# Attention in 64-row and 64x64 TensorE tiles, with compact states, slot-major tokens and a new instruction planner

## The chip, the cores and the metric

The kernel runs on one core of one Trainium2 chip. The metric is the device time of one execution in microseconds (us). The kernel before takes 210.27 us, the median of three runs (209.99 to 210.47).

Five engines work side by side, each through its own instructions in a fixed order: TensorE (PE; its weight loads are listed apart as PEld), VectorE (DVE), ScalarE (ACT), GpSimd (POOL) and SyncE (SP). In this kernel SP issues the loads of the inputs and the stores of the output, and POOL's queue issues the loads of the weights. Within one engine the instructions run in the order in which the program lists them, so an instruction whose input is late holds back every instruction behind it, whatever those need. (In the trace of before, shown below, a product that was ready at 36.99 us ran at 47.10 us for that reason.)

## The reference, cut to what matters

```python
# q, k, v, alpha: (B=4, H=8, S=768, D=48) fp32; alpha between 0.8 and 1.0
for t in range(S):
    state = alpha[:, :, t, :, None] * state + k_t (outer) v_t
    y[:, :, t] = q_t @ state
x = y as (B, 768 tokens, 384 columns)
h = relu(x.T @ w_tok1) @ w_tok2            # 768 -> 256 -> 768, along the tokens
u = x + h.T
out = u + relu(u @ w_ch1) @ w_ch2          # 384 -> 1536 -> 384, along the columns
```

## The kernel before: the parts that matter

The recurrence is computed in 12 chunks of 256 tokens, three to each of the four batches. A chunk is held as 128 pairs of tokens (64 pairs in each half), so that "slot 0" and "slot 1" are the even and the odd token of each pair. For each chunk the kernel forms running products of alpha (a cumulative sum of logarithms on TensorE, then exponentials on ACT, giving `E` and `IE`), scales q and k by them (`pkq`, `pkk`), transposes both, forms masked scores (`gtm`) and multiplies them by v ("y"). "K" is the product of k and v that updates the state, and "inter" adds to y what the state of earlier tokens gives. After three chunks the mixer of that batch can run: t1, t2, u, transposes of u, then 72 TensorE products c1, 72 products c2, the output tiles `o` and their stores.

The order is not written by hand. A planner on the host, a list scheduler, keeps a clock for each engine. It repeatedly takes the instruction that could start first, with a priority that decides between those that could start at about the same time. It knows the data's landing only through a model:

```python
    def run(self):                                     # class Plan
        ...
            if o.dma is not None:
                kind, dur, lead, tail = o.dma
                if kind == "w":                        # a weight transfer
                    s = max(st + lead, dma_w)
                    dma_w = s + dur
                    if dma_free > s:
                        dma_free += dur
                    else:
                        dma_free = max(dma_free, s) + 0.9 * dur
                else:                                  # a load of q, k, v or alpha
                    s = max(st + lead, dma_free)
                    dma_free = s + dur
                o.end = (dma_w if kind == "w" else dma_free) + tail
        ...
IN_NS, OUT_NS = 1450.0, 560.0
CLASSES = {... "vt": 5, "acqm": 2, "tmp": 2, "ss": 4, "rt": 24, "o": 4,
           "one": 4, "pair": 2}                        # PSUM: 4 single banks, 2 pairs
```

The operations that the change touches:

```python
    def tr(self, bank, cls, v):                        # q or k of one chunk: 8 transposes of 128x128
        for sl in range(2):
            for j in range(4):
                c = (sl * 4 + j) * 128
                self.pe.transpose(o[:, c : c + 128], s[:, sl, 2 * j : 2 * j + 2, :], self.idn)

    def evq(self, e, tpq, bq):                         # brings the two slots back into token order
        self.copy(e, self.t(tpq).rearrange("p j (t s) -> p s j t", s=2), ...)

    def kmm(self, kp, pkk, vb, nst):                   # two heads at a time: half of each result is unused
        ... self.bank(kp, hf)[:, 96 * j : 96 * j + 96], lhsT=kk[ph, sl, 2 * j : 2 * j + 2, :], ...

    def sadd(self, t, kp, s0, hf):                     # states are 384 columns wide
        self.nc.vector.tensor_tensor(self.t(t), self.bank(kp, hf)[:, 0:HD], self.t(s0), ALU.add)

    def inter(self, yp, tpq, s, hf):                   # acqm has zeroed the unused half
        for j in range(4):
            self.pe.matmul(self.bank(yp, hf)[:, 96 * j : 96 * j + 96],
                           lhsT=self.t(tpq)[:, j, hf * 128 : hf * 128 + 128],
                           rhs=self.t(s)[:, 96 * j : 96 * j + 96], ...)

    def store(self, o, b, i):
        self.nc.sync.dma_start(self.out[b, i * 128 : (i + 1) * 128, :], self.t(o))
```

## Time and profile before

| where in the trace of before | us |
|---|---|
| span of the profiled execution | 209.3 |
| start of the first channel product c1 (L702) | 58.7 |
| from there to the first t1 of batch 1 ("first mixer") | 27.4 |
| to the first t1 of batch 2 ("second mixer") | 48.2 |
| to the first t1 of batch 3 ("third mixer") | 39.5 |
| from there to the end of the span | 35.5 |

I read these five stages off the timeline of TensorE. The last four each hold one mixer's channel products (in before, 12 of the first mixer's 144 fall into the stage after it).

These lines are from the page of before. The first gives busy time and instructions. The others cut the span into 40 slices of 5.2 us; a digit is the busy share of a slice in tenths, PEclk is the clock granted to TensorE in tenths, and the last line is what the DMA engines moved.

```profile
PE 171.1 (82%) x2004; PEld 108.9 (52%) x2004; DVE 128.3 (61%) x200; ACT 98.0 (47%) x184; POOL 62.1 (30%) x66
PE   0367466119999999976888998999999999999993
PEclk9999976755999999999699999999999999999999
DMA  6999999999999997223001000211000112200042
GB/s 175 325 325 315 203 208 203 205 272 301 262 320 269 288 261 226 75 76 79 0 3 53 25 37 28 90 38 41 3 0 3 39 39 77 75 3 0 0 150 75
```

TensorE is nearly full from slice 10 on. Before that it is not, and two slices (37 to 47 us) have it at a tenth. The rate of the DMA engines falls from 325 to about 205 GB/s in slices 5 to 8, just when the weights move. Split by queue (the DMA view of the trace from 20.9 to 41.9 us), these slices hold so many packets, MB, and so much of the engines' time:

```profile
q0 software_dynamic: 3659, 3.05, 89.9%
q1 hardware_dynamic: 3225, 1.22, 33.1%
```

q0 carries the weights and q1 the loads. Both moved nearly the same number of packets, but a packet of weights is larger (about 830 against 380 bytes), so over these 21 us the loads are left with 58 GB/s of their 325. The 205 GB/s do not mean that the engines read less. The weights are counted by the bf16 bytes that are written (3.15 MB in all), while they are read as fp32: of the 25.17 MB that the page says were read from HBM, the 48 loads of 384 KB are 18.87, which leaves 6.29 MB for the weights. An estimate from these figures is 2 x 145 + 58, about 350 GB/s read. What fell is the share of the loads.

The granted clock is 5 to 7 tenths in slices 6 to 10, in and around the hole: the eight transposes at 46.13 us below take 1.04 us, those of a later, busy stage (113.57 us) 0.62 us.

Next, the chain of waits of before, followed back from the last instruction (start, length, what):

```profile
19.88 7.01 SPq L493
26.93 18.11 DMA qt<-in_q_dram
...
182.28 11.87 PE ps L702 x72
194.16 11.71 PE ps L707 x72
```

The chain waits for one q tile until 45.04 us. In its last part it is nothing but TensorE at 162 to 165 ns a product (11.71 us and 11.87 us over 72). No new order can shorten that part.

The timeline of before shows why so little happened from 37 to 47 us. Columns are start, length, engine and line, what was done, how many, and in brackets how long the engine had been idle and what ended that.

```profile
34.63 2.36 DVE L614 TENSOR_TENSOR gtm<-ps,mk 128x1024 bf16<-128x1024 f32 x2 [3.61 <-PE ps L606]
...
37.54 0.99 POOL L519 TENSOR_TENSOR at<-at 128x384 f32<-128x384 f32 x1 [11.08 <-DMA at<-in_alpha_dram]
...
43.32 0.99 POOL L545 TENSOR_TENSOR kt<-kt,at 128x384 f32<-128x384 f32 x1 [4.79 <-DMA kt<-in_k_dram]
...
44.27 1.80 POOL L553 TENSOR_TENSOR pkq<-qt,E 128x768 bf16<-128x768 f32 x1
...
46.03 2.13 POOL L553 TENSOR_TENSOR pkk<-kt,IE 128x768 bf16<-128x768 f32 x1
...
46.13 1.04 PE L586 MATMUL ps<-idn,pkq 128*128 128x128 bf16 x8 [6.33 <-POOL pkq L553]
...
46.41 2.57 DVE L553 TENSOR_TENSOR pkk<-kt,IE 128x768 bf16<-128x768 f32 x1
...
47.10 0.82 PE L650 MATMUL ps<-vb,gtm 64*128 64x48 bf16 x32
```

The masks of the third chunk are ready at 36.99 us (34.63 + 2.36), and its y (L650) needs nothing more that is late. It runs at 47.10. In TensorE's order it stands behind the q transposes of the fourth chunk. Those wait for POOL's `pkq`, and POOL stood for 11.08 and then 4.79 us on loads of the *fifth* chunk. The fifth chunk's alpha and k were put in front of the fourth chunk's work in POOL's order, because the planner believed that they would land earlier than they did.

The two `pkk` products at 46.03 and 46.41 show a second effect. VectorE's takes 2.57 us here; the shortest of its kind in this trace takes 0.94 us. It ends 0.82 us after POOL's. The Trainium skill, "SBUF — State Buffer", section "Who interferes with whom", says that a VectorE instruction with two inputs in SBUF contends with a GpSimd instruction that reads SBUF, and calls the port pair that they share an exclusive lock. These two lines agree with it for VectorE: its product ends about its own 0.94 us after POOL's, as if it had waited for POOL to finish. POOL's, at 2.13 us, is longer than the 1.80 us of its `pkq` too, but spans on POOL are rough.

### The profile page before, as it was taken

How to read it: one execution, taken by the hardware profiler on the slowest of the kernel's cores; microseconds unless marked ns; L12 is line 12 of the kernel's file. 1: busy time of each engine (PE TensorE's matmuls, PEld its weight loads, DVE VectorE, ACT ScalarE, POOL GpSimd, SP SyncE). 2: the span in 40 equal slices, each digit the busy share in tenths (PEclk: the TensorE clock that was granted, in tenths of full speed). 3: DMA queues.
4: the chain of work that ended last, by engine and by line, in shares of the span. 5: the costliest groups of instructions: out<-in, count | busy, mean ns of one | idle time of the engine just before them, and what ended most of it. 6: DMA issues, size and time to landing. Idle time of an engine off the chain costs nothing.

```text
span 209.3 us, 4761 instructions
## 1 busy us (share of the span) xinstructions
PE 171.1 (82%) x2004; PEld 108.9 (52%) x2004; DVE 128.3 (61%) x200; ACT 98.0 (47%) x184; POOL 62.1 (30%) x66
## 2 busy tenths in 40 slices
PE   0367466119999999976888998999999999999993
PEld 0246253016665666643545555656666666666551
DVE  2899973038999639289648968569645372800211
ACT  4474313516472750281577732146987301199200
POOL 4469700179372060075306031053800000000000
PEclk9999976755999999999699999999999999999999
DMA  6999999999999997223001000211000112200042
GB/s 175 325 325 315 203 208 203 205 272 301 262 320 269 288 261 226 75 76 79 0 3 53 25 37 28 90 38 41 3 0 3 39 39 77 75 3 0 0 150 75
DMA packets 57221, 27.04 MB, mean 129 GB/s; under 512 B 50416, under 2 KB 57200, under 8 KB 57200
## 3 DMA queue, kind: packets, MB, share of 16 engines
q1 hardware_dynamic: 53376, 23.60, 40.7%
q0 software_dynamic: 3824, 3.15, 9.3%
q8 instruction: 15, 0.25, 0.5%
q14 instruction: 6, 0.05, 0.1%
HBM read 25.17 MB, written 4.72 MB: 143 GB/s over the span
## 4 chain that ended last, share of the span: by engine, by line
PE 58%; DVE 15%; SPq 12%; DMA 9%; issue 3%; ACT 2%; DVEq 0%; ACTq 0%
PE ps L707 21%; PE ps L702 20%; SPq L493 12%; DMA qt<-in_q_dram 9%; PE ps L678 3%; PE ps L586 3%; DVE pkk L553 3%; DVE u L687 3%; DVE gtm L614 3%; PE ps L650 2%; PE ps L606 2%; PE ps L683 1%; PE ps L624 1%; PE ps L656 1%; DVE o L711 1%
## 5 line engine op out<-in xcount | busy, mean ns | idle before, releaser
L702 PE MATMUL ps<-ut,wc 128*128 128x384 bf16 x288 | 52.2, 331 | 1.1 <-ACT ut L590 0.3
L707 PE MATMUL ps<-wc,rt 128*128 128x384 bf16 x288 | 52.8, 326 | 0.0
L673 ACT ACTIVATE rt<-ps 128x384 bf16<-128x384 f32 x79 | 38.5, 494 | 13.9 <-PE ps L702 13.8
L702 PEld LDWEIGHTS <-wc 128*128 128x128 bf16 x288 | 27.2, 99 | 20.4 <-issue 3.9
L707 PEld LDWEIGHTS <-rt 128*128 128x128 bf16 x288 | 26.8, 98 | 16.8
L711 DVE TENSOR_TENSOR o<-ps,u 128x384 f32<-128x384 f32 x24 | 13.2, 555 | 32.6 <-PE ps L707 29.2
L614 DVE TENSOR_TENSOR gtm<-ps,mk 128x1024 bf16<-128x1024 f32 x24 | 28.7, 1217 | 3.7 <-PE ps L606 3.6
L590 ACT COPY tpq<-ps 128x1024 bf16<-128x1024 bf16 x11 | 14.4, 1309 | 13.7 <-PE ps L586 13.7
L574 POOL TENSOR_TENSOR acqm<-E,bm 128x16 f32<-128x16 f32 x12 | 9.0, 751 | 35.8 <-PE ps L683 12.0
L553 POOL TENSOR_TENSOR pkq<-qt,E 128x768 bf16<-128x768 f32 x6 | 10.8, 1806 | 20.8 <-ACT E L538 20.8
L590 ACT CAST x<-ps 128x384 bf16<-128x384 f32 x13 | 6.1, 485 | 22.9 <-PE ps L656 18.3
L586 PE MATMUL ps<-idn,pkq 128*128 128x128 bf16 x96 | 9.0, 249 | 8.1 <-POOL pkq L553 6.3
L687 DVE TENSOR_TENSOR u<-ps,x 128x384 bf16<-128x384 f32 x24 | 12.5, 551 | 4.5 <-PE ps L683 4.5
L678 PE MATMUL ps<-x,wt 128*128 128x384 bf16 x48 | 11.4, 373 | 4.4 <-ACT x L590 2.4
L532 PE MATMUL ps<-la,u 128*128 128x384 bf16 x12 | 4.8, 399 | 10.0 <-DVE u L473 6.0
L553 POOL TENSOR_TENSOR pkk<-kt,IE 128x768 bf16<-128x768 f32 x6 | 12.4, 2068 | 0.2 <-ACT IE L541 0.2
L606 PE MATMUL ps<-tpq,tpk 48*64 48x128 bf16 x384 | 10.9, 240 | 1.8 <-DVE tmp L638 1.0
L586 PEld LDWEIGHTS <-pkq 128*128 128x128 bf16 x96 | 7.2, 112 | 9.3 <-POOL pkq L553 6.4
L675 DVE TENSOR_SCALAR rt<-ps 128x384 bf16<-128x384 f32 x17 | 8.6, 556 | 5.4 <-PE ps L702 5.4
L592 DVE COPY tpk<-ps 128x1024 bf16<-128x1024 bf16 x11 | 7.6, 690 | 7.0 <-PE ps L586 7.0
L650 PE MATMUL ps<-vb,gtm 64*128 64x48 bf16 x384 | 8.0, 188 | 4.5 <-DVE gtm L614 4.4
L586 PE MATMUL ps<-idn,pkk 128*128 128x128 bf16 x96 | 9.0, 251 | 3.3 <-DVE pkk L553 2.0
(68 smaller groups left out, 225.8 us busy)
## 6 DMA issues: line engine op xcount, KB each, us to landing
at<-in_alpha_dram SPq DMA_DIRECT2D x12, 384.0 KB, 5.0
kt<-in_k_dram SPq DMA_DIRECT2D x12, 384.0 KB, 5.1
qt<-in_q_dram SPq DMA_DIRECT2D x12, 384.0 KB, 4.8
vt<-in_v_dram SPq DMA_DIRECT2D x12, 384.0 KB, 5.7
out_dram<-o SPq DMA_DIRECT2D x24, 192.0 KB, 1.9
wc<-in_moe_w_ch_dram POOLq DMA_DIRECT2D x3, 384.0 KB, 13.7
wc<-in_moe_w_ch_dram POOLq DMA_DIRECT2D x2, 576.0 KB, 17.9
wt<-in_moe_w_tok_dram POOLq DMA_DIRECT2D x2, 384.0 KB, 9.2
```

The costliest lines, as they stand in the source:

```text
L493: self.ins[id(v)] = self.nc.sync.dma_start(self.t(v), src)
L553: self.eng[e].tensor_tensor(dst[:, :, :, 0:D], src.rearrange("p h s d -> p s h d"), bass.AP(tensor=f.tensor, offset=f.offset, ap=[list(f.a ...
L586: self.pe.transpose(o[:, c : c + 128], s[:, sl, 2 * j : 2 * j + 2, :], self.idn)
L590: self.act.copy(d, s)
L606: self.pe.matmul(self.bank(gp, r)[hf * 64 : hf * 64 + 64, j * 128 : j * 128 + 128], lhsT=tk[r * 64 : r * 64 + D, sl * 4 + j, hf * 64 : hf ...
L614: self.nc.vector.tensor_tensor(self.t(gtm)[:, sl, :, :], pr, bass.AP(tensor=m.tensor, offset=m.offset, ap=[list(m.ap[0]), [0, 8], [1, 128] ...
L673: self.act.activation(d, s, AF.Relu)
L678: self.pe.matmul(self.bank(bank)[:, 0:HD], lhsT=self.wt1[:, kc, m * 128 : m * 128 + 128], rhs=self.t(x), start=(kc == 0), stop=(kc == NS - 1))
L687: self.nc.vector.tensor_tensor(self.t(u), self.bank(bank)[:, 0:HD], self.t(x), ALU.add)
L702: self.pe.matmul(self.bank(bank)[:, 0:HD], lhsT=self.wc1[:, kc, mc * 128 : mc * 128 + 128], rhs=self.t(ut)[:, kc, half * 384 : half * 384 ...
L707: self.pe.matmul(self.bank(bank)[:, 0:HD], lhsT=self.t(rts[mc][0])[:, i * 128 : i * 128 + 128], rhs=self.wc2[:, mc, :], start=(mc == 0), s ...
L711: self.nc.vector.tensor_tensor(self.t(o), self.bank(bank)[:, 0:HD], self.t(u), ALU.add)
```

## The change: its intent, and the diff

The stated intent is to do the attention products and transposes of the token pairs as 64-row or 64x64 TensorE tiles. A 64x64 tile of TensorE can compute one head alone, so that K no longer computes the unused cross terms of two heads. The states then need 192 columns instead of 384, and `acqm` (which zeroed the cross terms) goes. q stays in slot-major order, so its eviction from PSUM becomes contiguous. In return the tokens of x, and so of the output tiles, come in slot-major order: the rows of `wt1` and the columns of `wt2` are permuted, and each output tile is stored in two half-height transfers.

The diff holds more than that. It also replaces the planner. Cut to its core:

```diff
+    def landed(self, s, need):                 # a load advances at W_SHARE of its rate
+        ...                                    # while weights move
+            room = (b - t) * W_SHARE
     def run(self):
+        for _ in range(3):                     # plan, note when weights move, plan again
+            self.once()
...
-            if kind == "w": ...                # the model shown above
+            if kind == "w":
+                s = max(st + lead, dma_w); dma_w = s + dur
+                self.wnew.append((s, dma_w)); o.end = dma_w + tail
+            else:
+                dma_free = self.landed(max(st + lead, dma_free), dur)
+                o.end = dma_free + tail
+                    elif o.port and port_by != e and port > st and (e == "DVE" or e == "POOL"):
+                        st = port              # "port": products of VectorE and POOL exclude each other
...                                            # a model of TensorE's cold and warm clock; other slack
+W_SHARE = 0.19
-IN_NS, OUT_NS = 1450.0, 560.0
+IN_NS, OUT_NS = 1215.0, 560.0
-    "vt": 5, "acqm": 2, "tmp": 2, "ss": 4, "o": 4, "one": 4, "pair": 2,
+    "vt": 4,            "tmp": 3, "ss": 5, "o": 3,     # singles and pairs share the 8 PSUM banks
+WIDE = (0, 1, 2)        # batch 0: one 768-wide cumulative sum; no products P, k0a, q0r
...
     def tr(self, bp, v):
+        for c in range(8):
+            for hf in range(2):                # 16 transposes of 64x64
+                self.pe.transpose(o[:, c * 64 : c * 64 + 64], s[ph, c % 2, c - c % 2 : c - c % 2 + 2, :],
+                                  self.idn[ph, ph])
-    def inter(self, yp, tpq, s, hf): ...
+    def inter(self, yp, tpq, states, flip):    # one head per product, 64-row tiles
+                hf = r ^ flip                  # flip 0 and flip 1: each row tile changes the PSUM bank
+    def fence(self, e, yp):                    # a tiny read of PSUM between flip 0 and flip 1
+        self.copy(e, self.junk[e], self.pair(yp)[:, :, 7 * D - 1 : 7 * D + 1])
...
     def store(self, o, b, i):
+        dst = self.out[b, i * 128 : (i + 1) * 128, :].rearrange("(t s) d -> s t d", s=2)
+        for h in range(2):
+            self.nc.sync.dma_start(dst[h], self.t(o)[64 * h : 64 * h + 64, :])
```

The fence is there because of what the Trainium skill, "TensorEngine Tiling (Array Packing)", section "Restrictions and Gotchas", Gotcha 1, states: different row tiles cannot access the same PSUM bank at the same time. Leaving it out would be a race.

## The prediction

> **What bounds the kernel now.** In the chain of waits, the first 58.7 us hold almost no TensorE link: load issues by the sync queue to 26.9 us, then one DMA wait (a q tile) to 45.1 us. From 58.7 us on the chain is TensorE nearly without a break (L702 and L707, 41% of the span), with one bad stretch, 89 to 118 us, full of VectorE links.
>
> The prologue is a head-of-line loss more than a bandwidth limit. In the timeline the third chunk's masks end at 37.0 us, but its y product (L650) runs at 47.1: in TensorE's order it stands behind the fourth chunk's q transposes, whose input POOL made only at 44.27, after sitting (L519 at 37.5, L545 at 43.3) on loads of the *fifth* chunk. Those are late because the weights move too: the 40-slice row gives 325 GB/s before and about 205 from 21 to 42 us. The Trainium skill, "DMA: Bandwidth & Descriptors", on arbitration, says each engine round-robins between queues; the trace agrees.
>
> **What the change does.** The built order shows that the planner has changed, not only the tiles. Before the first channel product TensorE now needs only chunks 0 to 3; before, chunk 3 had landed by about 30 us. ACT's second ut eviction stands behind one load of chunk 4 (37.5 us before). Batch 0 loses nine products (P, k0a, q0r; 0.55 to 1.1 us each). After chunk 3 come transposes, t1, ht, t2 on a cold clock, then about 7 us of VectorE (six u at 0.55, q0r, qq, a tpq). I expect the first channel product (L702 before) at about 43 us instead of 58.7: minus 15 us, nearly all critical.
>
> TensorE per chunk, warm: transposes 2 x 0.45 us become 2 x 0.32 (20 ns for 64 columns, interpolated between y, 16 ns at 48, and K, 28 ns at 96); K 0.44 to 0.5; inter 0.34 to 0.26; one more change of tiling. "TensorEngine Tiling (Array Packing)", Key Properties, says a mode change drains; here three products cost 0.59 instead of 0.49 us after attention: 0.1 us each. Net about 0.2 us x 8 chunks: minus 1.5 us.
>
> VectorE: state adds 0.55 to 0.33, multiplies 0.64 to 0.38, tpq eviction 1.30 (strided) to 0.69, on ACT 1.31 to 1.02; acqm (9 us of POOL) goes; fences come (0.1 us each, plus waiting). Some 8 us less, of which perhaps 4 count, in the second mixer: from its t1 to the next batch's t1 before spent 48 us, against 39.5 for the following one. Eight shared PSUM banks help there too.
>
> Costs: permuting wt2 (two ACT copies, hidden), split stores (tail 0.4 us longer), TensorE stalls at the fence (0 to 0.5 us a chunk).
>
> Sum: 210.3 - 15 - 1.5 - 4 = 189.8; I say **189 us**, range **181 to 198**. Chances: faster 0.97, same 0.02, slower 0.01.
>
> **What would show it.** Right: first channel product at 40 to 47 us; y of the third chunk before 36; second mixer 40 to 45 us; transposes about 20 ns apart, under 0.35 us a group; POOL busy under 45 us; final channel stretch as before. Wrong: TensorE waiting on chunk 4's loads before the first channel product; transposes no faster; TensorE gaps before inter's second half.
>
> **What would make it wrong.** If weights (wt1 in two half-height transfers) or chunk 3's loads land later, the prologue gain shrinks to 8 us. If denser VectorE work or the fences stall TensorE, 5 us return. If the second mixer runs as the third, 183 us.

## The result, and the profile after

The median is 191.77 us (190.72 to 191.84, four runs) against 210.16 us for before (four runs by then). The ratio is 0.911, with a 95% interval of 0.908 to 0.915. Ratios in this document compare the runs of one kernel with the runs of the other in the same rounds, so they are not quite the ratio of the medians that I quote. Executions over 1.5% slower than the fastest of the same kernel are left out of the means.

The same five stages in both traces:

| | before | after | difference |
|---|---|---|---|
| first c1 starts at | 58.7 | 40.9 | -17.8 |
| first mixer | 27.4 | 32.5 | +5.1 |
| second mixer | 48.2 | 40.6 | -7.6 |
| third mixer | 39.5 | 39.0 | -0.5 |
| last stage | 35.5 | 37.1 | +1.6 |
| span | 209.3 | 190.1 | -19.2 |

From the page of after:

```profile
PE 164.0 (86%) x2489; PEld 101.7 (53%) x2489; DVE 112.8 (59%) x197; ACT 101.2 (53%) x200; POOL 35.9 (19%) x43
PE   0578578769999988977999999989999999999990
PEclk9999999978999999999999999999999999999997
DMA  5999999999999998999100123110001132000243
GB/s 156 322 320 270 240 209 207 205 203 270 283 295 247 288 299 229 298 264 269 47 3 3 41 54 75 41 47 5 3 0 40 46 86 71 12 3 0 65 100 83
```

The hole at 37 to 47 us is gone. Slices are 4.75 us here, so TensorE is nearly full from 43 us on, and the granted clock dips in two slices only, besides the last. The rate of about 205 GB/s while the weights move has stayed. The loads did not become faster; the order stopped depending on the late ones.

From the timeline of after, the lines that answer to those of before:

```profile
30.53 0.57 PE L617 MATMUL ps<-vb,gtm 64*128 64x48 bf16 x32
...
39.65 0.52 ACT L605 ACTIVATE lf<-at 128x384 f32<-128x384 f32 x1 [2.11 <-DMA at<-in_alpha_dram]
...
40.08 0.78 ACT L683 COPY ut<-ps 128x768 bf16<-128x768 bf16 x1
...
40.91 4.11 PE L794 MATMUL ps<-ut,wc 128*128 128x384 bf16 x15 [1.24 <-ACT ut L683]
```

The third chunk's y runs at 30.53 instead of 47.10 us. The first channel product still waits a little for a load: ACT's `ut` copy stands behind its own first step on the next batch's alpha.

The chain of waits of after:

```profile
20.53 19.10 DMA at<-in_alpha_dram
40.91 4.11 PE ps L794 x15
...
64.83 6.69 DMA at<-in_alpha_dram
...
161.54 11.87 PE ps L794 x72
173.41 11.71 PE ps L799 x72
```

The last two lines are the same as before to the digit. The wait at 64.83 is new. It lies in the first mixer, the stage that became 5.1 us longer. But only a third of these 5.1 us is waiting. These two lines give the first mixer in before and in after, from the view of busy time by stretch: its bounds, its length, the busy time of PE, PEld, DVE, ACT and POOL with the count of instructions, the granted clock, and the DMA engines' share and GB/s:

```profile
58.68:86.12 27.44, 27.40 (x322) 17.06 (x317) 21.05 (x36) 11.59 (x22) 8.22 (x8) 1.00 0.93 255
40.91:73.42 32.51, 30.83 (x468) 18.24 (x468) 22.88 (x39) 23.09 (x49) 7.43 (x9) 0.95 1.05 270
```

TensorE was busy for 27.40 of 27.44 us and is now busy for 30.83 of 32.51, so 1.7 us are waiting and 3.4 us are longer work. Both stages hold 132 channel products. The first 15 of them in after, at a lower granted clock, took 4.11 us (274 ns each, where the last 72 took 165): that is about 1.7 us. The other 1.7 us or so are attention products that stood before the first c1 and now stand behind it; y of the fourth chunk, for one, runs at 44.96. (The two halves of the 3.4 us are estimates from these figures.) At the first t1 of batch 1 the gain is thus 12.7 us (86.12 less 73.42), not 17.8. The timeline of after shows the waiting, and one wait of the second mixer:

```profile
71.61 0.52 ACT L605 ACTIVATE lf<-at 128x384 f32<-128x384 f32 x1 [3.55 <-DMA at<-in_alpha_dram]
72.04 0.14 ACT L683 COPY junkACT<-ps 128x4 f32<-128x4 f32 x1
...
72.23 0.28 PE L617 MATMUL ps<-ss,tpq 48*128 48x48 bf16 x8 [1.68 <-ACT junkACT L683]
...
85.70 0.56 DVE L803 TENSOR_TENSOR o<-ps,u 128x384 f32<-128x384 f32 x1 [1.79 <-DMA out_dram<-o]
...
86.32 0.66 PE L794 MATMUL ps<-ut,wc 128*128 128x384 bf16 x3 [1.45 <-DVE o L803]
```

TensorE now starts its first mixer so early that it meets the loads, which keep the DMA engines busy until about 90 us (19 slices). The fence of one chunk (`junkACT`, 0.14 us of work) was planned on ACT behind a step that needs the next alpha tile. The tile lands at 71.6 us, and TensorE stands 1.68 us. This is in the first mixer. In the second, VectorE stands 1.79 us for a store to release one of the three output tiles, and TensorE 1.45 us behind it.

The operations themselves did become cheaper. These are groups of instructions by line and shape (count, busy us, mean ns of one, idle time before them and its releasers), first of before, then of after:

```profile
L553 DVE TENSOR_TENSOR pkk<-kt,IE 128x768 bf16<-128x768 f32 x6 | 10.8, 1794 | 0.0
L638 DVE TENSOR_TENSOR tmp<-ps,ss 128x384 f32<-128x384 f32 x16 | 8.8, 551 | 0.7 <-PE ps L624 0.4
L641 DVE TENSOR_TENSOR ss<-tmp,acqm 128x384 bf16<-128x384 f32 x12 | 7.7, 643 | 0.8
```

```profile
L658 DVE TENSOR_TENSOR pkk<-kt,IE 128x768 bf16<-128x768 f32 x8 | 8.3, 1033 | 4.7 <-ACT IE L642 4.5 <-ACT IE L639 0.2
L724 DVE TENSOR_TENSOR tmp<-ps,ss 128x192 f32<-128x192 f32 x16 | 5.6, 351 | 0.6 <-ACT x L683 0.4
L727 DVE TENSOR_TENSOR ss<-tmp,E 128x192 bf16<-128x192 f32 x13 | 5.5, 425 | 0.3
```

The two state operations fell from 551 and 643 ns to 351 and 425 ns. The `pkk` product of the first lines did not change in shape; that it fell from 1794 to 1033 ns is taken up below. For the transposes, look at how far apart two neighbouring groups start, before and then after:

```profile
113.57 0.62 PE L586 MATMUL ps<-idn,pkk 128*128 128x128 bf16 x8 [0.70 <-DVE pkk L553]
114.03 0.61 PE L586 MATMUL ps<-idn,pkq 128*128 128x128 bf16 x8
```

```profile
94.48 0.41 PE L673 MATMUL ps<-idn,pkq 64*128 64x64 bf16 x16
94.73 0.40 PE L673 MATMUL ps<-idn,pkk 64*128 64x64 bf16 x16
```

Eight large transposes take 0.46 us from start to start, sixteen small ones 0.25 us. In the trace's single records the small ones mostly start in pairs, one product 3 or 4 ns after the other and 25 or 26 ns from pair to pair, 16 ns on average; the large ones start 55 or 56 ns apart. (The lengths in these lines include the latency of the last product.) The stores became dearer, 588 ns an issue instead of 332, and twice as many. The fields after the count are the shortest, median and longest issue in ns, in before and in after:

```profile
L514 SPq DMA_DIRECT2D out_dram<-o x24: 332/332/1287, 76.7 to 206.5; - x24
```

```profile
L597 SPq DMA_DIRECT2D out_dram<-o x48: 466/588/1583, 76.3 to 187.0; - x48
```

From this result alone one would say that the prediction came true for the reasons it gave: the time is 191.77 against 189, and the stages moved as foreseen. The experiments show that a good part of those reasons was wrong.

### The profile page after: what moved, and what is told of

It is laid out like the page before. It is cut to its first block, busy times and chain, and to the rows that moved or that the text cites. A ratio compares the mean times of both kernels' runs of the same rounds, so it can differ in the third digit from the quotient of the medians.

```text
span 190.1 us, 5770 instructions
## 1 busy us (share of the span) xinstructions
PE 164.0 (86%) x2489; PEld 101.7 (53%) x2489; DVE 112.8 (59%) x197; ACT 101.2 (53%) x200; POOL 35.9 (19%) x43
## 4 chain that ended last, share of the span: by engine, by line
PE 62%; DMA 16%; SPq 10%; DVE 6%; ACT 2%; issue 2%; DVEq 0%; ACTq 0%
PE ps L794 26%; PE ps L799 21%; DMA at<-in_alpha_dram 14%; SPq L562 10%; PE ps L617 7%; PE ps L770 3%; DMA out_dram<-o 2%; DVE u L779 2%; PE ps L775 2%; PE ps L673 2%; DVE pkk L658 1%; DVE pkq L658 1%; DVE o L803 1%; PE ps L786 1%; DVE gtm L698 1%
## 5 line engine op out<-in xcount | busy, mean ns | idle before, releaser
L765 ACT ACTIVATE rt<-ps 128x384 bf16<-128x384 f32 x93 | 45.1, 490 | 10.9 <-PE ps L794 10.6
L698 DVE TENSOR_TENSOR gtm<-ps,mk 128x1024 bf16<-128x1024 f32 x24 | 28.5, 1218 | 2.3 <-PE ps L617 2.2
L779 DVE TENSOR_TENSOR u<-ps,x 128x384 bf16<-128x384 f32 x24 | 12.7, 552 | 2.0 <-PE ps L775 2.0
L602 POOL TENSOR_TENSOR at<-at 128x384 f32<-128x384 f32 x6 | 6.0, 996 | 33.8 <-DMA at<-in_alpha_dram 22.2
L658 DVE TENSOR_TENSOR pkq<-qt,E 128x768 bf16<-128x768 f32 x10 | 11.0, 1097 | 1.0 <-ACT E L636 1.0
L658 DVE TENSOR_TENSOR pkk<-kt,IE 128x768 bf16<-128x768 f32 x8 | 8.3, 1033 | 4.7 <-ACT IE L642 4.5
L775 PE MATMUL ps<-ht,wt 128*128 128x384 bf16 x48 | 9.8, 326 | 0.4 <-ACT ht L765 0.4
L673 PE MATMUL ps<-idn,pkk 64*128 64x64 bf16 x192 | 5.5, 202 | 5.4 <-DVE pkk L658 3.1
L658 POOL TENSOR_TENSOR pkq<-qt,E 128x768 bf16<-128x768 f32 x2 | 3.6, 1810 | 31.8 <-PE ps L673 31.8
L617 PEld LDWEIGHTS <-tpk 48*64 48x64 bf16 x384 | 7.2, 121 | 3.8 <-issue 1.3
L658 POOL TENSOR_TENSOR pkk<-kt,IE 128x768 bf16<-128x768 f32 x4 | 7.2, 1811 | 10.0 <-ACT IE L642 10.0
L765 ACT ACTIVATE ht<-ps 128x384 bf16<-128x384 f32 x7 | 3.4, 490 | 10.5 <-PE ps L770 10.5
```

The costliest lines, as they stand in the source:

```text
L617: return self.pe.matmul(out, lhsT=lhsT, rhs=rhs, start=start, stop=stop, skip_group_check=True)
L658: self.eng[e].tensor_tensor(self.t(dst)[:, :, :, 0:D], self.t(src).rearrange("p h s d -> p s h d"), bass.AP(tensor=f.tensor, offset=f.offs ...
L673: self.pe.transpose(o[:, c * 64 : c * 64 + 64], s[ph, c % 2, c - c % 2 : c - c % 2 + 2, :], self.idn[ph, ph])
L698: self.nc.vector.tensor_tensor(self.t(gtm)[:, sl, :, :], self.pair(gp).rearrange("p a (j t) -> p (a j) t", t=128), bass.AP(tensor=m.tensor ...
L765: self.act.activation(d, s, AF.Relu)
L775: self.pe.matmul(self.bank(bank)[:, 0:HD], lhsT=self.wt2[:, kc, i * 128 : i * 128 + 128], rhs=self.t(hts[kc]), start=(kc == 0), stop=(kc = ...
```

## The experiments

Theory ORDER: the gain is the new planner's, above all its view of when loads land. Rival TILES: the cheaper operations carry a large part of it, in the mixers. (The expectations were written before each run; where one names a theory in other words, the rival of ORDER is the one that credits the operations or one single rule of the planner.) The runs were made in four sessions, each on one chip beside its own runs of before (medians 210.49, 209.88, 209.94 and 210.11 us). I compare kernels of different sessions through their ratios to before. For the differences between changed kernels I also name the stages of their profiles.

### e1: the new planner with the old operations

```diff
- class Plan of before; "one": 4, "pair": 2; IN_NS 1450
+ class Plan of after; 8 shared PSUM banks; IN_NS 1215; port=True on the products of DVE and POOL
  (transposes, K, states of 384 columns, acqm, inter, token-major x, one store, o 4: as before)
```

> The old products, transposes, states and stores, planned by the new planner (its view of when loads land, the eight shared PSUM banks, the port rule). Theory ORDER (most of the 19 us is the order of instructions in the first 60 us): first channel product at 40 to 46 us instead of 58.7, 195 to 199 us in all, at least two thirds of the gain. Rival WORK (the gain is the smaller work of the 64-row tiles, the compact states and the shorter evictions): 205 to 210 us.

Measured: 189.73 us, ratio 0.900 (0.895 to 0.906), correct. One of the four runs, the profiled one, was slow (193.6 us), so I use its stages only roughly: first c1 at 41.9 us. The planner alone thus carries more than the whole gain. The old operations under it are 1.2% faster than the change as given (0.9004 over 0.9112), and the two intervals do not overlap. TILES falls in its plain form. The lead of e1 over after is about what the split stores cost: after with one store a tile (e7, whose result is wrong) has 0.898 (0.892 to 0.903), which overlaps with e1.

### e2: the old planner with the new operations

```diff
- class Plan of after; 8 shared PSUM banks
+ class Plan of before; "one": 4, "pair": 2
  (all operations, WIDE, stores: as after)
```

> All operations of the changed kernel, planned by the old planner (old view of the loads, four single PSUM banks and two pairs). ORDER: TensorE stands again behind chunk 4's q transposes before the first channel product, which comes at 48 to 58 us; 199 to 207 us in all. WORK: 191 to 195 us.

Measured: 219.25 us, ratio 1.041 (1.035 to 1.047), correct. Both expectations missed it by far. The first c1 starts at 61.8 us and the second mixer takes 51.8 us. The timeline of e2 shows the same disease as before had, on ACT and POOL:

```profile
40.06 0.52 ACT L550 ACTIVATE lf<-at 128x384 f32<-128x384 f32 x1 [11.56 <-DMA at<-in_alpha_dram]
40.11 0.99 POOL L547 TENSOR_TENSOR at<-at 128x384 f32<-128x384 f32 x1 [9.35 <-DMA at<-in_alpha_dram]
```

This run says that the new operations gain nothing under the old planner. It does not measure the operations alone, because the new transposes write to a pair of banks, and the old split offers only two pairs to six kinds of work.

### e3: before, with one number changed

```diff
+LATE = {4: 12000.0, 5: 12000.0, 6: 12000.0}
-  ... dma=("i", IN_NS, 1100.0, 650.0))
+  ... dma=("i", IN_NS, 1100.0, 650.0 + LATE.get(n, 0.0)))
```

The planner of before is told that the loads of chunks 4 to 6 (counted from 0) land 12 us later than it thinks. Nothing else changes.

> The kernel before with one number changed: its planner is told that the loads of chunks 4 to 6 land 12 us later than it thought; not one operation differs. ORDER: the third chunk's y product runs at 32 to 38 us instead of 47, the first channel product at 42 to 48 us, 196 to 201 us in all. WORK: 208 to 211 us.

Measured: 212.65 us, ratio 1.009 (1.003 to 1.016), correct. Half of ORDER's expectation came true: the first c1 starts at 47.6 us instead of 58.7, and the third chunk's y at 35.6. The total did not follow. The first mixer took 38.9 us instead of 27.4, which gave back the 11 us: TensorE was busy for 4.6 us more there, in part at a lower granted clock (0.91 in this stage), and idle for 6.9. The timeline of e3 shows the idle part:

```profile
59.09 0.56 DVE L520 TENSOR_TENSOR at<-at 128x384 f32<-128x384 f32 x1 [7.51 <-DMA at<-in_alpha_dram]
...
60.17 1.12 PE L703 MATMUL ps<-ut,wc 128*128 128x384 bf16 x3 [6.87 <-DVE rt L676]
```

VectorE stood 7.51 us on the next alpha load, so the ReLU evictions behind it did not run, and TensorE stood 6.87 us with channel products it could have done. A constant lateness moved the wait to the next load. The start of the mixer is therefore not a measure of the gain: an earlier start is worth something only if the order after it is also right about the loads.

### e4: after, without the wide form of batch 0

```diff
-WIDE = (0, 1, 2)
+WIDE = ()
```

> The changed kernel with batch 0 prepared as the other batches (no cumulative sums of 768 columns). If the wide form matters for the first channel product, that comes 2 to 3 us later and the whole is 193.5 to 195.5 us. If the first channel product waits for loads (its second ut eviction stood behind chunk 4's alpha load), at most 1 us is lost: 191 to 193 us.

Measured: 190.83 us, ratio 0.907 (0.900 to 0.913), correct. The interval overlaps with that of after, so faster or equal is unclear. The wide form, to which the prediction gave part of its earlier start, gains nothing that these runs show; the first c1 is even earlier without it (38.6 against 40.9 us, of which the first mixer gives back 1.6).

### e5: e1, with the old split of PSUM

```diff
-  (singles and pairs from the same 8 banks)
+    "one": 4, "pair": 2,
```

> As e1 (new planner, old tiles), but with the old division of PSUM, four single banks and two pairs, in place of eight shared banks. If sharing the banks is what shortens the stretch from batch 1's t1 to batch 2's t1 (48 us before, 43 in e1), that stretch is 46 us or more and the whole 193 to 197 us. If not, 189 to 191.5 us as e1. First channel product at 40 to 46 us either way.

Measured: 192.70 us, ratio 0.916 (0.910 to 0.923), correct. Without the shared banks the kernel is 1.8% slower than e1 (0.9165 over 0.9004), about 3 us. In which stage these are lost can't be said, as the profile of e1 is a slow one. But the second mixer takes 40.9 us here, not the 46 or more that would make shared banks the cause of its gain.

### e6: e1, with the old view of the loads

```diff
-        dma_free, dma_w = 2400.0, 0.0
+        dma_free, dma_w = 0.0, 0.0
-                    dma_free = self.landed(max(st + lead, dma_free), dur)
-                    o.end = dma_free + tail
+                    s = max(st + lead, dma_free)
+                    dma_free = s + dur
                     ...                      # and the old rule for weights
-IN_NS, OUT_NS = 1215.0, 560.0
+IN_NS, OUT_NS = 1450.0, 560.0
  (weights at 300 instead of 285)
```

> As e1, but with the old rule for when loads land (weights push back only loads planned after them) in the new planner. LOADS (the view of when loads land is what gains the 17 us of the prologue): first channel product at 48 us or later, or the same loss a little later as in e3; 197 to 208 us. If the other rules of the new planner carry the gain: 189 to 193 us.

Measured: 202.55 us (202.49 to 202.60), ratio 0.963 (0.958 to 0.968), correct. In the new planner this view of the loads is worth 13 us, two thirds of what e1 gains. The loss lies in the start: the first c1 is at 55.9 us (41.9 in the slow profile of e1) and the first t1 of batch 1 at 83.3 (73.0), while the second mixer stays at 41.8 us. From the timeline of e6, its first c1, and from its chain of waits:

```profile
55.94 0.66 PE L760 MATMUL ps<-ut,wc 128*128 128x384 bf16 x3
```

```profile
34.57 11.64 DMA vt<-in_v_dram
```

### e7: after, with one store for each output tile

```diff
-        dst = self.out[b, i * 128 : (i + 1) * 128, :].rearrange("(t s) d -> s t d", s=2)
-        for h in range(2):
-            self.nc.sync.dma_start(dst[h], self.t(o)[64 * h : 64 * h + 64, :])
+        self.nc.sync.dma_start(self.out[b, i * 128 : (i + 1) * 128, :], self.t(o))
```

The result is wrong: the tokens are stored in slot-major order.

> The changed kernel with one store a tile instead of two half-height ones; rows of the output then stand in a wrong order, on purpose. If the two stores cost the end (from batch 3's t1 to the end 37.1 us, before 35.5), that stretch is 35.4 to 35.8 us, and the stall of VectorE behind stores in the second mixer shrinks: 189 to 190.5 us. If not, 191.3 to 192 us.

Measured: 188.81 us, ratio 0.898 (0.892 to 0.903), with one of four runs slow (191.53 us). TensorE, VectorE, ScalarE and GpSimd run their instructions in the same order as in after, so this comparison is free of a new plan. The split stores cost 1.5% (0.8976 over 0.9112), about 3 us. Of that, 1.6 us lies in the last stage, 35.5 instead of 37.1 us: after the last `o` the span goes on for 2.8 us in before (206.46 to 209.3) and for 4.4 us in after (185.71 to 190.1). The Trainium skill, "DMA: Bandwidth & Descriptors", section "Rules for kernel authors", advises against two transfers to disjoint halves of the partitions and says that they serialize. The runs agree with the advice: two halves for each tile gained nothing and made the end 1.6 us longer. Whether the halves serialize, they do not show.

### e8: after, with the large transposes

```diff
-        for c in range(8):
-            for hf in range(2): ... 64x64 transposes
+            self.pe.transpose(o[:, c * 128 : c * 128 + 128], s[:, c % 2, c - c % 2 : c - c % 2 + 2, :], self.idn)
```

> The changed kernel with 8 transposes of 128 rows where it has 16 of 64, evicted with the same count of elements. If the 64-row transposes are worth TensorE time on the critical path (0.45 against 0.32 us a group, 24 groups, 18 of them in the stretches that TensorE bounds): 193 to 195 us, transposes 0.43 to 0.47 us a group. If that time is not critical: 191.2 to 192.3 us.

Measured: 192.68 us, ratio 0.916 (0.911 to 0.921), correct. That is 0.5% above after, with overlapping intervals: unclear. It fell between the two expectations. The small transposes are cheaper by 0.20 us a group (0.45 in e8's trace less 0.25), 24 groups in all, about 5 us of TensorE work as an estimate; TensorE's busy time on the two pages differs by 1.5 us (165.5 and 164.0). By the medians, 0.9 us shows in the total.

### e9: e1, without the port rule

```diff
-  port=True
```

> As e1 (new planner, old tiles), but the planner is not told that VectorE and POOL hinder each other (the port rule). If that rule is what shortens the stretch from batch 1's t1 to batch 2's (48 us before, 41 to 43 with the new planner): 45 us or more, POOL busy over 50 us, 193 to 197 us in all. If not: 41 to 43.5 us and 189 to 191.5 us in all.

Measured: 192.10 us, ratio 0.914 (0.909 to 0.918), correct, 1.5% above e1. The first c1 is late (47.1 us), and so is the first t1 of batch 1 (75.8 us, 73.0 in the slow profile of e1). The second mixer takes 39.5 us, so the port rule is not the cause of its gain either.

### e10: after, with x back in token order

```diff
-    evq: contiguous; weights permuted; two stores
+    evq: "p f j (t s) -> p f j s t" (strided); weights as they are; one store
```

> The changed kernel with the x tiles back in token order: one store a tile, no permuted token weights, but a strided eviction of tpq (1.3 us again instead of 0.69 on VectorE and 1.01 on ACT); 64-row tiles and compact states stay. If slot-major order loses more by its stores than it gains by the eviction: from batch 3's t1 to the end 35.5 us, and 188.5 to 190.5 us in all. If the eviction is worth more: 192 us or more.

Measured: 192.16 us (190.51 to 194.78), ratio 0.912 (0.906 to 0.918), correct. The strided eviction of q takes 1.304 us on ACT instead of 1.012. The last stage became 1.6 us shorter, as in e7, but the first c1 came at 44.4 us and the second mixer took 42.2 us. The plan had been dealt anew and lost elsewhere what the stores gained. Neither expectation was met.

### e11: the version that the earlier runs point to

```diff
  (e10, and:)
-    ... "o": 3,
+    ... "o": 4,
-WIDE = (0, 1, 2)
+WIDE = ()
-            "E": ([128, 776], F32), "IE": ([128, 768], F32), ...
+            "E": ([128, 392], F32), "IE": ([128, 384], F32), ...
```

The wide form goes, which frees the memory for a fourth output tile, and each output tile has one store. The 64x64 transposes, the compact states and the new planner stay.

> As e10, without the wide preparation of batch 0 and with four output tiles instead of three (the room comes from E and IE). If both are of use as e4 hinted: 187 to 189.5 us, correct, faster than the changed kernel and than e1. If e4's microsecond was chance: 189 to 190.5 us.

Measured: 186.93 us (185.37 to 187.68), ratio 0.889 (0.882 to 0.895), correct. It is the fastest kernel and beats before and after (0.911) clearly. Against e1 (0.900, in another session) it gains 1.3%, about 2.5 us; the intervals touch there, while all its runs are below all of e1's (189.47 us and up).

### e12: after, with four output tiles

```diff
-    ... "rt": 24, "o": 3,
+    ... "rt": 23, "o": 4,
```

> The changed kernel with four output tiles instead of three, as before the change; the room is taken from the ReLU tiles, 23 instead of 24. If the third tile's reuse (VectorE waited 1.8 us on a store near 85 us, and TensorE 1.4 us on VectorE) is a wait that the change brought in: that wait is gone, batch 1's t1 to batch 2's takes 39 to 39.8 us instead of 40.6, and the whole 190 to 191 us. If the time is lost elsewhere all the same: 191.3 to 192.3 us.

Measured: 191.52 us, ratio 0.911 (0.904 to 0.917), correct: no difference from after. The second mixer became shorter as expected (39.4 us), but the first c1 came 1.0 us later (41.95), although the order of the instructions up to that point is the same in both kernels. The alpha tile that it waits for landed at 39.6 us in after and at 40.7 in e12. Landing times of loads thus differ by about 1 us between executions, and a smaller difference in the start of one profile means nothing.

### What the experiments settle, and what they don't

Settled: the planner carries the gain (e1, e2). About 13 us of it is its view of the loads (e6). The split stores cost about 3 us (e7). Without shared banks or without the port rule e1 loses about 3 us each (e5, e9); but not in the stage that was expected, and each is also a plan dealt anew, so how much of these 3 us is the rule itself is not shown.

Not settled: why the second mixer fell from 48 to about 41 us. It stays at 39.5 to 41.8 us when the load view, the shared banks or the port rule is taken away singly, with the old operations in place; so it is neither the operations nor any one of these three. What remains is the model of TensorE's clock, the slack between nearly equal choices, a few buffer counts, or a combination. One lead, though no run tests it: VectorE's `pkk` product, which can be held up by POOL, took 1794 ns on average in before and 1669 in e2, both under the old planner, and 950 to 1175 ns in every kernel with the old operations under the new one (e1, e5, e6, e9), even without the port rule. e3 shows only that lateness of the loads alone doesn't do it (49.0 us).

Also not settled is how much of e11's 2.5 us over e1 is due to the cheaper operations. Every edit makes the planner deal a new order; e4, e10 and e12 moved single stages by 1 to 3.5 us that way. The third mixer is the best witness, as few loads reach into it. With the new planner it took 39.3 to 40.6 us in the kernels with all old operations (e5, e6, e9), and 38.2 to 39.1 us in those with the new transposes, products and states (after, e4, e7, e10, e11, e12). e8, with only the transposes undone, took 39.7. That is consistent with about 1 us a mixer under the new planner. Under the old one it is the other way: 39.5 us in before, 40.6 in e2.

## Why the prediction was right or wrong

The total came out as said: 189 us with a range of 181 to 198, measured 191.77. Point by point:

1. *"The prologue is a head-of-line loss more than a bandwidth limit"* was right. With the DMA rate unchanged at about 205 GB/s while the weights move, the first c1 moved from 58.7 to 40.9 us; "about 43" was said, and "minus 15" was -17.8. e6 confirms the mechanism: with the old view of the loads it is back at 55.9 us. *"Batch 0 loses nine products"* did not matter for it (e4: 38.6 us without the wide form).
2. *"All critical"* was the weak step. The sum counted the earlier start of the first c1 as gained, with no term for the stage after it, but the first mixer grew by 5.1 us. Of these, 1.7 us are waiting, about 1.7 us a lower granted clock in the first channel products, and about 1.7 us attention work that had only moved behind the first c1 (the prediction itself had seen that *"TensorE now needs only chunks 0 to 3"* before it). By the first t1 of batch 1 the gain was 12.7 us and not 17.8. The same happened in the extreme in e3, where 11 us of earlier start were worth nothing. The signs of this were on the list of what would be "wrong" or make it wrong: TensorE waited for chunk 4's loads before the first channel product (1.24 us, through ACT), and it waited at a fence before inter's second half (1.68 us). Each was named, but neither was put into the sum.
3. *"TensorE per chunk ... minus 1.5 us"* had about the right durations: transposes 16 ns apart on average (0.25 us over 16) where 20 were said. The third mixer, where this should show alone, gained 0.5 us.
4. *"VectorE ... some 8 us less, of which perhaps 4 count, in the second mixer ... Eight shared PSUM banks help there too"* had the right place and the wrong cause. The second mixer took 40.6 us, within the 40 to 45 that were named, a gain of 7.6 us. But with the *old* operations under the new planner it takes 39.5 to 41.8 us (e5, e6, e9), and with the old split of PSUM 40.9 (e5). VectorE's busy time in that stage fell from 35.0 us to 28.5 in after, and also to 28.0 in e9, which has all the old operations: what VectorE shed there, the order shed, not the narrower states.
5. *"Split stores (tail 0.4 us longer)"* was too small: the last stage is 1.6 us longer, and the whole cost is about 3 us (e7).
6. *"POOL busy under 45 us; final channel stretch as before"* were right: 35.9 us, and 11.87 and 11.71 us in both.

The errors cancelled. The prologue and the second mixer brought 6.4 us more than the 19 that the sum gave them (17.8 + 7.6 - 19), and the first mixer and the tail took 6.7 us that it did not contain. What the prediction got wrong in kind is point 4: it had read from the built order that "the planner has changed, not only the tiles", and then still credited the mixers' gain to the operations.

## What to carry to other kernels

When a change rewrites both the operations and the rule that orders them, compare the two halves under the same rule: here the old operations under the new planner were faster than the whole change, by about what the split stores cost, and the pieces that paid could then be picked out for a better kernel. On engines that work in order, the planner's knowledge of when loads land can be worth more than cheaper instructions, and a correction by a constant only moves the wait to the next load. An earlier start of a stage counts only together with the length of the stage after it, since a plan can move work from one to the other. A planned order also changes with every edit, by 1 to 3 us a stage here, so a small gain of one edit is believed only when the stage where it should show agrees.

## What the Trainium skill lacked or had wrong

- "DMA: Bandwidth & Descriptors", section "Queues, rings and completion order", says that an engine goes round its queues packet by packet. It does not say what is left to a queue whose packets are the smaller ones. Here the loads moved 325 GB/s alone and 58 GB/s beside the weights, with 3225 packets of about 380 bytes against 3659 of about 830. Nor does it say that issuing slows down: in before, single issues on SyncE's queue grew from about 1.15 us to as much as 7.0 us from the time at which the weights began to move.
- No page that I read says how much the landing of the same load differs between executions. Between two kernels with the same order up to that point, the first channel product differed by 1.0 us.
